# Operand preparation moved about in a fused attention and expert kernel: a second raw-weight buffer, earlier GpSimd sums, other places for copies out and late forms, six staging tiles

## The chip, the cores and the metric

The kernel runs on one core of a Trainium2 chip, as one program that is launched once. The metric is the device time of that launch in microseconds. The kernel before was run three times: 1815.36, 1820.99 and 1821.14 us, median 1820.99.

The engines are named as in the profile: PE is TensorE (matrix products), DVE is VectorE, ACT is ScalarE, POOL is GpSimd, and SP is SyncE, which here issues nearly all DMAs. Each engine works through its own instruction list in order.

## The reference

A gated linear attention makes x, and a mixture of experts over x makes the output. Every expert is applied to every token; the gate is normalised over rows and columns in eight iterations.

```python
# attention: q, k, v, a_re, a_im are [4, 8, 768, 48]
for t in range(S):
    S_re, S_im = ar * S_re - ai * S_im + k[t] (x) v[t], ar * S_im + ai * S_re
    y[t] = q[t] @ S_re
x = y, reordered to [3072, 384]

# experts: N = 3072 tokens, D = 384, E = 8, F = 1024
P = exp(x @ w_gate - max)
for _ in range(8):
    P /= P.sum(1, keepdims=True) + 1e-9
    P /= P.sum(0, keepdims=True) + 1e-9
    P *= N / E
out = sum over e of P[:, e:e+1] * (relu(x @ w1[e]) @ w2[e])
```

## The kernel before, in words

**Stages.** Phase 1 (to about 541 us) makes x in twelve blocks of 256 tokens by the attention, and runs experts 0 and 1 on each block behind it (matmul lines L234 and L207 to L209). A short tail to 645 us (`phase2a`) ends those experts, does the first three iterations of the gate, and prepares the first two weight sets for phase 2b. Phase 2b, from 645 us to the end, runs experts 2 to 7 over all tokens, and nearly all of the change is there.

**The steps of phase 2b.** The 3072 tokens are four groups u of 768. The six experts have 48 hidden chunks of 128; three chunks make one weight set t, so there are 16 sets, and 64 steps n, one for each pair of group and set: u = n // 16, and m is the number of the step within its group. Even groups walk the sets upward, odd ones downward.

**One step.** The first layer is a scheme of 15 block products in place of 18 (`prod`, matmul lines L1052 to L1054, three matmuls of 384 columns each, in a high and a low part for precision). Its token operands are 15 forms (`P1` to `P15`: sums and differences of token blocks), and its weight operands are in four tiles `wa`, `wb`, `wc`, `wd`. Products go to PSUM banks X, Y, Z, V and P (X and P take turns in one pair of buffers, Y, Z and V in another). A finished bank is copied by ACT (`copy`, L1062) or added by DVE (`add`, L1065) into the partial results "11", "12", "21", "22" (that one stays in its bank), "31" and "32". Then come the relus: ACT writes the high part (L1070), DVE the low part `hl` (L1071). Between the products stand the 18 units of the second layer, which belong to the step before (`unit`, matmul lines L1005 to L1007, three matmuls each). `fill(s)`, s from 0 to 14, stands after each product and holds units, jobs for that place (`todo`), jobs of the late forms (`xjobs`), and one job of `fin`. A step has 99 matmuls.

**The banks of the second layer.** The units write six accumulators (`po`) for the token chunks k = 0 to 5. When an expert ends for a group, each accumulator is added into the output tile `oa` by a job of `finish` (by ACT at L984 and L986 for the first expert of a group, by DVE at L988 otherwise), which is put in `fin`; the last expert's job also stores the tile (L990: to `od`, or to the output). `fin` gives up one job at each of the fills 0 to 7, 10 and 11.

**Weights.** In the group u = 0 the sets are made on the fly: `raw_w` loads raw weights (L819, 1152 KB), `sums` forms their sums with 12 groups of operations on GpSimd (L828), and `prep_w` splits each tile into a high part (ACT, L865) and a low part (DVE, L869) and stores it to DRAM (L871). There is one raw tile and one sum tile. In step m the raw load of set m + 2 is issued at fill 6, the sums of set m + 2 at fill 7; the tiles of set m + 1 are split at fills 0 to 5, `wa` (from sums) at 3. Groups u of 1 or more reload the finished sets (`load_set`, L851), all four tiles at fill 0.

**Forms.** The forms of groups 0 and 1 are made during phase 1 (`forms_early`, through two staging tiles `xst`), those of groups 2 and 3 during the steps of group u - 1 (`forms_late`, in steps of n = 16 on and 32 on). A list of jobs does it: `plain` (eight DMAs from `x_d` to `xf`, L767), loads (two DMAs each, L739, into `xb` and `xt`), `full` (DVE, L743), sums (DVE, L749), high part (ACT, L755), low part and store (DVE and SP, L760 and L761). Late jobs are taken at fills 1, 3 and 5 of a step. `swap` (L810) reloads one form of the next group as soon as the last product of the old one has used it.

**Ends of a step.** The relu of "31" for the third chunk is put off into the next step: `carry` (L1092) runs ACT's and DVE's part after the first product.

Notation in code: `SUB` = 256, `TH` = 384 (a half of a group's tokens), `C` = 384, `TRI` = 3, `NS` = 3, `NT` = 16, `NU` = 4. The order of instructions on each engine is that in which the code is written and the fills are emptied; DMAs of SP are issued in that order, and at most eight are under way at a time.

Of the kernel before, what the change touches and what calls it, by code (L numbers as in the profile page):

```python
# [18 lines left out]
CH = 128  # L19
# [53 lines left out]
class Net:  # L73
# [707 lines left out]
    def forms_early(self):  # L781
        tmp, G = self.tmp, NCT * NCH
        T = [tmp.tile([128, G, CH], F32, tag="t1", name=f"xt{k}", bufs=5).rearrange("p (j s) t -> p j (s t)", j=2) for k in range(5)]
        sq = tmp.tile([128, 2, G, CH], F32, tag="sq", name="xst", bufs=1).rearrange("p a (j s) t -> p a j (s t)", j=2)
        temps = [T[3][:, 0], T[3][:, 1], T[4][:, 0]]
# [12 lines left out]
    def forms_late(self, u, pool):  # L798
        n = [0]

# [4 lines left out]
        return self.forms(u, lambda c, j: pool.tile([128, TH], F32, tag=f"xb{c}{j}", name=f"xb{c}{j}_{u}"), temp,  # L805
# [6 lines left out]
    def raw_w(self, t):  # L812
        raw = self.raw = self.wr.tile([128, TRI, 2 * C], F32, tag="raw", name=f"raw{t}")
# [8 lines left out]
    def sums(self, t):  # L822
        G = self.nc.gpsimd
        R = self.raw.rearrange("p f (c d) -> p f c d", d=128)
        s = self.sum = self.wr.tile([128, 11, 128], F32, tag="sum", name=f"sum{t}")
# [17 lines left out]
    def ring(self, t):  # L843
        W = self.W[t] = {nm: self.wp.tile([128, 2, 6, 128], F32R, tag="w", name=f"{nm}{t}_{self.nring}") for nm in ("wa", "wb", "wc", "wd")}
        self.nring += 1
        return W

    def load_set(self, t):
        W = self.ring(t)
        for q, nm in enumerate(("wa", "wb", "wc", "wd")):  # L850
            self.nc.sync.dma_start(W[nm].bitcast(F32).rearrange("p a b c -> p (a b c)"), self.wd[t][:, q])  # L851

    def prep_w(self, t):
        nc, V, A = self.nc, self.nc.vector, self.nc.scalar
        R = self.raw.rearrange("p f (c d) -> p f c d", d=128)
        W, s = self.ring(t), self.sum
        parts = {}

        def part(name, nm, pieces):
            w = W[nm]  # L860
            po = [([w[:, h, k] if k is not None else w[:, h].rearrange("p (a b) d -> p a b d", a=2) for h in range(2)], src) for k, src in pieces]

            def hi():
                for o, src in po:
                    A.activation(o[0], src, AF.Copy)  # L865

            def lo():
# [3 lines left out]
                nc.sync.dma_start(self.wd[t][:, q], w.bitcast(F32).rearrange("p a b c -> p (a b c)"))  # L871

            parts[name] = (hi, lo)

        part("wd", "wd", [(None, R[:, 1:3, 3:6])])
        part("wc", "wc", [(slice(0, 5), R[:, 0, 1:6]), (5, R[:, 1, 0])])
        part("wa", "wa", [(slice(0, 6), s[:, 0:6])])
        part("wb", "wb", [(5, R[:, 1, 2]), (slice(0, 5), s[:, 6:11])])
        return parts

    def phase2a(self, c2):
# [7 lines left out]
        self.W, self.X, self.nring = {}, {}, 0  # L889
# [14 lines left out]
        self.raw_w(0)  # L904
        self.sums(0)
# [5 lines left out]
        for k in range(HEAD):  # L911
# [3 lines left out]
            if k < 2:  # L915
                prepare(k)
                self.raw_w(k + 1)
            if k == 0:
                self.sums(1)
        more(len(todo))  # L920
        self.moe.send((None, None, None))

    def phase2b(self, c2):
# [22 lines left out]
        def rescale(u, k):  # L946
            tt = tile_of(u, k)
            A.activation(oa[tt], oa[tt], AF.Copy, scale=self.P[:, tt, 2:3])

        def early(u, k):  # L950
# [8 lines left out]
            def job():  # L959
                r = o if u == 0 else oa[tt]  # L960
# [14 lines left out]
        def finish(u, e, k):  # L975
# [4 lines left out]
            def job():  # L980
                if e == e0:
                    oa[tt] = self.xa.tile([128, C], F32, tag=f"oa{k}", name=f"oa{tt}")
                    if u == 0:
                        A.activation(oa[tt], p, AF.Copy)  # L984
                    else:
                        A.activation(oa[tt], p, AF.Copy, scale=self.P[:, tt, e:e + 1])  # L986
                else:
                    V.scalar_tensor_tensor(oa[tt], p, self.P[:, tt, e:e + 1], oa[tt], ALU.mult, ALU.add)  # L988
                if e == e1:
                    nc.sync.dma_start(self.od[k] if u == 0 else self.out[tt * CH:tt * CH + CH, :], oa[tt])  # L990
# [21 lines left out]
        for n, (u, t) in enumerate(steps):  # L1012
# [54 lines left out]
            def hh(i, j, src):  # L1067
                t = [self.hp.tile([128, TH], F32R, tag=f"h{q}{i}{j}", name=f"h{q}{i}{j}_{n}") for q in "hl"]
                h[i, j] = t
                A.activation(t[0], src, AF.Relu)  # L1070
                return lambda: V.scalar_tensor_tensor(t[1], src, 0.0, t[0].bitcast(F32), ALU.max, ALU.subtract)  # L1071

            def fill(s):
# [5 lines left out]
                if u and s in (1, 3, 5) and m < NT - 1 and xjobs:  # L1079
# [3 lines left out]
                if s < 8 or s in (10, 11):  # L1083
# [31 lines left out]
            l01 = hh(0, 1, c["12"])  # L1115
# [10 lines left out]
            hh(1, 1, bank["X"])()  # L1126
# [3 lines left out]
            l00 = hh(0, 0, c["11"])  # L1130
# [4 lines left out]
            l10 = hh(1, 0, c["21"])  # L1135
# [4 lines left out]
            l21 = hh(2, 1, c["32"])  # L1140
# [10 lines left out]
        carry.pop(0)()  # L1151
# [180 lines left out]
```

## Time and profile before

| what | value |
|---|---|
| runs before | 1815.36, 1820.99, 1821.14 us (median 1820.99) |
| profiled execution | 1818.91 us, span 1817.1 us, mean granted TensorE clock 0.987 |
| end of phase 1, start of phase 2b | about 541 us, 645.72 us |
| step 0 of phase 2b | 645.72 to 660.66 us |
| group u = 0, steps 1 to 15 | 660.66 to 948.06 us |
| u = 1, u = 2, u = 3 | from 948.06, 1234.81 and 1522.15 us |
| matmuls | 11774, PE busy 1742.1 us |
| DMA | 346.03 MB, mean 190 GB/s |

How to read it: steps are told apart by their last product's matmuls, and the start of a step is that of its first product. A row of waits gives the instruction that waited, by its engine, tile and line, then `<-` and what released it, then the sum, the number and the longest of these waits. A row of windows gives the start and end, the length, the busy time (and count of instructions) of PE, weight loads, DVE, ACT and POOL, then the granted clock, the share of the DMA engines and GB/s. A row of the timeline gives start, duration, engine, line, operation, tiles and, in brackets, idle time and its releaser.

### The profile page before, as it was taken

The numbers are of one execution on the slowest core, as the hardware profiler recorded it, in microseconds if no ns is written. First come the engines' busy times: TensorE is split into PE (matmuls) and PEld (weight loads), VectorE is DVE, ScalarE is ACT, GpSimd is POOL, SyncE is SP. The second block draws the span as 40 slices with busy tenths as digits, with TensorE's granted clock in tenths as the row PEclk, the third lists the DMA queues.
The fourth block names the chain that finished last, engine by engine and source line by source line (L and its number), as shares of the span: only waits on it lengthen the run. The fifth ranks groups of instructions, "written<-read, shape, count | busy, mean of one in ns | idle before, by whom it ended". The sixth has DMA issues, their size and how long they took to land.

```text
span 1817.1 us, 31284 instructions
## 1 busy us (share of the span) xinstructions
PE 1742.1 (96%) x11774; PEld 1690.6 (93%) x11774; DVE 1289.1 (71%) x2710; ACT 746.5 (41%) x1673; POOL 219.3 (12%) x360
## 2 busy tenths in 40 slices
PE   6999999999999989999999999999999999999998
PEld 4888899999999978899998999999999999999998
DVE  7888999998886678877765566655566655556554
ACT  7544444554544544444432433332433333333332
POOL 3101111111110144335310000000000000000000
PEclk9999999999999999999999999999999999999999
DMA  7435444543457855666667666667656746455550
GB/s 218 120 92 144 115 100 125 161 111 110 117 152 237 333 219 202 236 231 235 243 231 243 227 236 246 211 203 251 222 209 217 233 176 226 174 183 210 192 195 31
DMA packets 160831, 346.03 MB, mean 190 GB/s; under 512 B 15264, under 2 KB 101536, under 8 KB 160672
## 3 DMA queue, kind: packets, MB, share of 16 engines
q1 hardware_dynamic: 155264, 334.03, 53.8%
q0 software_dynamic: 4608, 9.52, 2.1%
q8 instruction: 95, 1.56, 0.3%
q14 instruction: 64, 0.52, 0.1%
q10 hardware_dynamic: 800, 0.39, 0.1%
HBM read 232.53 MB, written 98.70 MB: 182 GB/s over the span
## 4 chain that ended last, share of the span: by engine, by line
PE 74%; DVE 10%; DMA 6%; POOL 4%; ACT 3%; issue 2%; SPq 1%; DVEq 0%; ACTq 0%; POOLq 0%
PE ph L234 9%; PE po L1005 9%; PE po L1007 9%; PE po L1006 9%; POOL sum L828 4%; DMA raw<-in_w_dram 4%; PE po L207 3%; PE po L209 3%; PE po L208 3%; PE X L1052 3%; PE X L1054 3%; PE X L1053 3%; PE sp L577 2%; PE Y L1052 2%; PE Y L1053 2%; PE Y L1054 2%
## 5 line engine op out<-in xcount | busy, mean ns | idle before, releaser
L1005 PE MATMUL po<-wd,hh 128*128 128x384 f32 x768 | 258.3, 336 | 7.4 <-DVE oa L988 3.4
L1007 PE MATMUL po<-wd,hl 128*128 128x384 f32 x768 | 257.9, 336 | 0.0
L1006 PE MATMUL po<-wd,hh 128*128 128x384 f32 x768 | 257.8, 336 | 0.0
L234 PE MATMUL ph<-xh,w 128*128 128x256 f32 x1152 | 228.5, 283 | 4.5 <-ACT hf L247 3.3
L234 PEld LDWEIGHTS ph<-xh,w 128*128 128x128 f32 x1152 | 187.4, 191 | 5.7 <-ACT hf L247 3.8
L246 ACT ACTIVATE hh<-ph 128x256 fp32r<-128x256 f32 x192 | 73.2, 381 | 208.7 <-PE ph L234 207.9
L234 PE MATMUL ph<-xl,w 128*128 128x256 f32 x576 | 155.1, 284 | 1.3 <-DVE xl L647 1.3
L1005 PEld LDWEIGHTS po<-wd,hh 128*128 128x128 f32 x768 | 145.1, 189 | 8.7 <-DVE oa L988 4.0
L1007 PEld LDWEIGHTS po<-wd,hl 128*128 128x128 f32 x768 | 145.0, 189 | 0.4 <-DVE hl L1071 0.2
L1006 PEld LDWEIGHTS po<-wd,hh 128*128 128x128 f32 x768 | 145.0, 189 | 0.0
L207 PE MATMUL po<-w,hh 128*128 128x384 f32 x384 | 141.4, 368 | 0.6 <-ACT yst L212 0.5
L1005 PE MATMUL po<-wc,hh 128*128 128x384 f32 x384 | 130.1, 339 | 6.6 <-ACT oa L986 3.3
L209 PE MATMUL po<-w,hl 128*128 128x384 f32 x384 | 131.1, 342 | 2.7 <-DVE hl L248 2.6
L208 PE MATMUL po<-w,hh 128*128 128x384 f32 x384 | 130.4, 339 | 0.0
L1007 PE MATMUL po<-wc,hl 128*128 128x384 f32 x384 | 129.9, 338 | 0.0
L539 POOL DMA_DIRECT2D qs<-z x144 | 77.0, 541 | 438.0 <-issue 84.3
L1006 PE MATMUL po<-wc,hh 128*128 128x384 f32 x384 | 129.7, 338 | 0.0
L234 PEld LDWEIGHTS ph<-xl,w 128*128 128x128 f32 x576 | 106.8, 191 | 1.8 <-DVE xl L647 1.7
L1070 ACT ACTIVATE hh<-X 128x384 fp32r<-128x384 f32 x64 | 31.5, 492 | 186.2 <-PE X L1054 186.2
L248 DVE TENSOR_TENSOR hl<-hf,hh 128x256 fp32r<-128x256 f32 x192 | 81.0, 423 | 27.8 <-ACT hf L247 26.6
L828 POOL TENSOR_TENSOR sum<-raw 128x128 f32<-128x128 f32 (+1 forms) x96 | 66.3, 721 | 230.5 <-DMA raw<-in_w_dram 145.3
L988 DVE SCALAR_TENSOR_TENSOR oa<-po,P,oa 128x384 f32<-128x384 f32 x120 | 72.9, 612 | 19.6 <-PE po L1007 19.6
(1818 smaller groups left out, 4458.9 us busy)
## 6 DMA issues: line engine op xcount, KB each, us to landing
wd<-wd SPq DMA_DIRECT2D x58, 768.0 KB, 5.7
wa<-wd SPq DMA_DIRECT2D x42, 768.0 KB, 4.3
wb<-wd SPq DMA_DIRECT2D x42, 768.0 KB, 5.7
wc<-wd SPq DMA_DIRECT2D x42, 768.0 KB, 4.4
xP<-xf SPq DMA_DIRECT2D x60, 384.0 KB, 4.8
raw<-in_w_dram SPq DMA_DIRECT2D x12, 1152.0 KB, 7.9
wd<-wc SPq DMA_DIRECT2D x16, 768.0 KB, 3.5
wd<-wa SPq DMA_DIRECT2D x16, 768.0 KB, 3.9
```

Source lines behind the costliest of these rows:

```text
L207: nc.tensor.matmul(po[k], hh[:, s], w2h, start=f == 0, stop=False)
L208: nc.tensor.matmul(po[k], hh[:, s], w2l, start=False, stop=False)
L209: nc.tensor.matmul(po[k], hl[:, s], w2h, start=False, stop=f == NF - 1)
L234: nc.tensor.matmul(ph, w[:, k, ct * 128:ct * 128 + 128], x[:, ct, :], start=q == 0, stop=q == len(terms) - 1)
L248: nc.vector.tensor_tensor(hl, hf, hh.bitcast(F32), ALU.subtract)
L828: G.tensor_tensor(o, a, b, op)
L1005: nc.tensor.matmul(po[k], hh[:, s], w2[0], start=c == 1, stop=False)
L1006: nc.tensor.matmul(po[k], hh[:, s], w2[1], start=False, stop=False)
L1007: nc.tensor.matmul(po[k], hl[:, s], w2[0], start=False, stop=c == NF)
L1052: nc.tensor.matmul(ps, w[:, 0, k], x[:, 0], start=start, stop=False, skip_group_check=True)
L1053: nc.tensor.matmul(ps, w[:, 0, k], x[:, 1], start=False, stop=False, skip_group_check=True)
L1054: nc.tensor.matmul(ps, w[:, 1, k], x[:, 0], start=False, stop=True, skip_group_check=True)
```

## The change

1. `forms_early` stages through six tiles: the two of `xst` and four that lie in tiles of the attention's input pool.
2. `forms_late` keeps the six loaded blocks in one tile `xb`. During u = 0, when there are no late forms, the slot of that tile holds the raw weights of the odd sets from t = 3 on: a second raw buffer. The raw weights of set 1 go to the place of the output tile, before that is used.
3. Raw weights are asked for a step sooner: sets 0 and 1 at the start of phase 2a, set 2 there after the sums of set 1, set 3 in step 0, and set m + 3 at fill 5 of step m. The sums of set m + 2 are issued at fill 5 of step m (7 before).
4. `prep_w` for set m + 1: the high part of `wd` is made at fill 12 of the step before, and the others stand one fill earlier than before. A slot of the ring of weight tiles is taken where its high part is made.
5. `oa` is one tile for the six chunks of a group, not one for each chunk.
6. `carry`: the relu of "31" is issued after the copy of "11" in place of before that of "12", and its low part after the first `add`.
7. `fin` gives up a job at fill 12 as well.
8. Late forms: no job at fills 1, 3 and 5 of a group's first step (m = 0); the first three jobs (`plain` and two loads) come at its fill 14, the rest from m = 1 on.

```diff
     def forms_early(self):
...
+        qk = self.ain.tile([128, 2, G, CH], F32, tag="qk", name="xsu", bufs=1).rearrange(...)
+        z = self.ain.tile([128, 2, G, ZW], F32, tag="z", name="xsv").rearrange(...)[...]
+        stages = [t[:, a] for t in (sq, qk, z) for a in range(2)]
...
-            return sq[:, n[1] % 2].bitcast(F32R)
+            return stages[n[1] % len(stages)].bitcast(F32R)
...
     def forms_late(self, u, pool):
+        x = pool.tile([128, 2 * NCT, TH], F32, tag="xb", name=f"xb{u}")
...
-        return self.forms(u, lambda c, j: pool.tile([128, TH], F32, tag=f"xb{c}{j}", name=f"xb{c}{j}_{u}"), temp,
+        return self.forms(u, lambda c, j: x[:, 2 * c + j], temp,
...
-    def raw_w(self, t):
-        raw = self.raw = self.wr.tile([128, TRI, 2 * C], F32, tag="raw", name=f"raw{t}")
+    def raw_w(self, t, pool=None):
+        if t == 1:
+            raw = self.xa.tile([128, 2 * NS, C], F32, tag="oa", name=f"raw{t}").rearrange(...)
+        elif pool is None:
+            raw = self.wr.tile([128, TRI, 2 * C], F32, tag="raw", name=f"raw{t}")
+        else:
+            raw = pool.tile([128, 2 * NCT, TH], F32, tag="xb", name=f"raw{t}").rearrange(...)
+        self.raw[t] = raw
...
         self.raw_w(0)
+        self.raw_w(1)
         self.sums(0)
...
                 prepare(k)
-                self.raw_w(k + 1)
             if k == 0:
                 self.sums(1)
+                self.raw_w(2)
...
             if u == 0 and 1 <= m < NT - 1:
-                parts = self.prep_w(m + 1)
-                for nm, a, b in (("wd", 0, 1), ("wc", 1, 2), ("wa", 3, 4), ("wb", 4, 5)):
-                    todo.setdefault(a, []).append(parts[nm][0])
+                for nm, a, b in (("wd", None, 0), ("wc", 0, 1), ("wa", 2, 3), ("wb", 3, 4)):
+                    if a is not None:
+                        todo.setdefault(a, []).append(parts[nm][0])
                     todo.setdefault(b, []).append(parts[nm][1])
+            if n == 0:
+                self.raw_w(3, xb)
             if u == 0 and m + 2 < NT:
-                if m:
-                    todo.setdefault(6, []).append(lambda t=m + 2: self.raw_w(t))
-                todo.setdefault(7 if m else 0, []).append(lambda t=m + 2: self.sums(t))
+                parts = self.prep_w(m + 2)
+                todo.setdefault(12, []).append(parts["wd"][0])
+                todo.setdefault(5 if m else 0, []).append(lambda t=m + 2: self.sums(t))
+                if m and m + 3 < NT:
+                    todo.setdefault(5, []).append(lambda t=m + 3: self.raw_w(t, xb if t % 2 else None))
...
-                if u and s in (1, 3, 5) and m < NT - 1 and xjobs:
+                if u and s in (1, 3, 5) and 0 < m < NT - 1 and xjobs:
                     xjobs.pop(0)()
                     if len(xjobs) > 3 * (NT - 2 - m):
                         xjobs.pop(0)()
-                if s < 8 or s in (10, 11):
+                if u and m == 0 and s == 14 and xjobs:
+                    for _ in range(3):
+                        xjobs.pop(0)()
+                if s < 8 or s in (10, 11, 12):
                     if fin:
                         fin.pop(0)[1]()
...
             prod("P1", "X", True)
             copy("12", "X")
-            while carry:
-                carry.pop(0)()
             fill(0)
             prod("P2", "Y", True)
             copy("11", "Y")
+            l20 = carry.pop(0)() if carry else None
             fill(1)
             prod("P4", "X")
             add("11", "X")
+            if l20:
+                l20()
             fill(2)
```

SP's list where the steps 15, 16 and 17 meet, before (`xP` are swapped forms, `xf` and `x_d` the forms and blocks in DRAM, `od` the stored output tiles):

```order
L810 DMA xP_1_11863<-xf_160 128x768
L767 DMA xf_161<-x_d_93 128x3x128 x8
L739 DMA xb_2_11909<-x_d_93 128x3x128
L739 DMA xt_1_11910<-x_d_93 128x3x128
L739 DMA xb_2_11928<-x_d_93 128x3x128
L739 DMA xt_2_11929<-x_d_93 128x3x128
L990 DMA od_166<-oa_9453 128x384
L990 DMA od_167<-oa_9467 128x384
L990 DMA od_168<-oa_9480 128x384
L851 DMA wa_16_12056<-wd_156 128x1536
```

and of the change:

```order
L814 DMA xP_1_11860<-xf_160 128x768
L1003 DMA od_166<-oa_9462 128x384
L1003 DMA od_167<-oa_9462 128x384
L1003 DMA od_168<-oa_9462 128x384
L1003 DMA od_163<-oa_9462 128x384
L767 DMA xf_161<-x_d_93 128x3x128 x8
L739 DMA xb_11869<-x_d_93 128x3x128
L739 DMA xt_1_12034<-x_d_93 128x3x128
L739 DMA xb_11869<-x_d_93 128x3x128
L739 DMA xt_2_12037<-x_d_93 128x3x128
L861 DMA wa_64_12050<-wd_156 128x1536
```

The eight plain DMAs and the four loads have moved behind four stores of finished tiles, the fourth of which (`od_163`, chunk 0) belongs to fill 12 of step 16.

DVE's list at the start of step 16, before (L1071 is the low part of a relu, L743 a `full` of the late forms, L988 a copy out, L1065 an `add`):

```order
L1071 SCALAR_TENSOR_TENSOR hl_15_11868<-31_15_11732,hh_15_11867 128x384
L1065 TENSOR_TENSOR 11_16_11896<-11_16_11896,X_11882 128x384
L743 TENSOR_TENSOR xb_2_11909<-xb_2_11909,xt_1_11910 128x384
L988 SCALAR_TENSOR_TENSOR oa_9453<-po_0_3_11595,P,oa_9453 128x384
L988 SCALAR_TENSOR_TENSOR oa_9467<-po_0_4_11606,P,oa_9467 128x384
L743 TENSOR_TENSOR xb_2_11928<-xb_2_11928,xt_2_11929 128x384
L988 SCALAR_TENSOR_TENSOR oa_9480<-po_0_5_11615,P,oa_9480 128x384
L1065 TENSOR_TENSOR 31_16_11923<-31_16_11923,X_11882 128x384
```

and DVE's list from the late part of step 16 into step 17 with the change (L1091, L1001 and L1082 are the lines that were L1071, L988 and L1065):

```order
L1091 SCALAR_TENSOR_TENSOR hl_16_11985<-11_16_11892,hh_16_11984 128x384
L1001 SCALAR_TENSOR_TENSOR oa_9462<-po_0_0_11638,P,oa_9462 128x384
L1082 TENSOR_TENSOR 32_16_11929<-32_16_11929,V_12004 128x384
L1091 SCALAR_TENSOR_TENSOR hl_16_11997<-21_16_11919,hh_16_11996 128x384
L1082 TENSOR_TENSOR 31_16_11909<-31_16_11909,V_12004 128x384
L1091 SCALAR_TENSOR_TENSOR hl_16_12011<-32_16_11929,hh_16_12010 128x384
L1001 SCALAR_TENSOR_TENSOR oa_9462<-po_0_1_11649,P,oa_9462 128x384
L743 TENSOR_TENSOR xb_11869<-xb_11869,xt_1_12034 128x384
L743 TENSOR_TENSOR xb_11869<-xb_11869,xt_2_12037 128x384
L1001 SCALAR_TENSOR_TENSOR oa_9462<-po_0_2_11662,P,oa_9462 128x384
L1082 TENSOR_TENSOR 11_17_12064<-11_17_12064,X_12040 128x384
L1091 SCALAR_TENSOR_TENSOR hl_16_12022<-31_16_11909,hh_16_12021 128x384
```

Both `full` have moved from step 16, one on each side of two copies out, to the start of step 17, ahead of that step's first `add`, and the copy out of chunk 0 has moved from step 17 into step 16.

More of the change, by code (lines that the diff above doesn't have):

```diff
@@ L823, in sums @@
         G = self.nc.gpsimd
-        R = self.raw.rearrange("p f (c d) -> p f c d", d=128)
-        s = self.sum = self.wr.tile([128, 11, 128], F32, tag="sum", name=f"sum{t}")
+        R = self.raw[t].rearrange("p f (c d) -> p f c d", d=128)
+        s = self.sum[t] = self.wr.tile([128, 11, 128], F32, tag="sum", name=f"sum{t}")
         def tt(o, a, b, op=ALU.subtract):
@@ L841, in sums, with ring, part @@
         tt(s[:, 10], s[:, 10], s[:, 5])
-    def ring(self, t):
-        W = self.W[t] = {nm: self.wp.tile([128, 2, 6, 128], F32R, tag="w", name=f"{nm}{t}_{self.nring}") for nm in ("wa", "wb", "wc", "wd")}
+    def ring(self, t, nm):
+        W = self.W.setdefault(t, {})
+        W[nm] = self.wp.tile([128, 2, 6, 128], F32R, tag="w", name=f"{nm}{t}_{self.nring}")
         self.nring += 1
-        return W
+        return W[nm]
     def load_set(self, t):
-        W = self.ring(t)
         for q, nm in enumerate(("wa", "wb", "wc", "wd")):
-            self.nc.sync.dma_start(W[nm].bitcast(F32).rearrange("p a b c -> p (a b c)"), self.wd[t][:, q])
+            self.nc.sync.dma_start(self.ring(t, nm).bitcast(F32).rearrange("p a b c -> p (a b c)"), self.wd[t][:, q])
     def prep_w(self, t):
         nc, V, A = self.nc, self.nc.vector, self.nc.scalar
-        R = self.raw.rearrange("p f (c d) -> p f c d", d=128)
-        W, s = self.ring(t), self.sum
+        R = self.raw[t].rearrange("p f (c d) -> p f c d", d=128)
         parts = {}
-        def part(name, nm, pieces):
-            w = W[nm]
-            po = [([w[:, h, k] if k is not None else w[:, h].rearrange("p (a b) d -> p a b d", a=2) for h in range(2)], src) for k, src in pieces]
+        def part(nm, pieces):
+            po = []
             def hi():
+                w = self.ring(t, nm)
+                po.extend(([w[:, h, k] if k is not None else w[:, h].rearrange("p (a b) d -> p a b d", a=2) for h in range(2)], src()) for k, src in pieces)
                 for o, src in po:
@@ L870, in lo @@
                 q = ("wa", "wb", "wc", "wd").index(nm)
[L871 to L878, printed above, removed]
+                nc.sync.dma_start(self.wd[t][:, q], self.W[t][nm].bitcast(F32).rearrange("p a b c -> p (a b c)"))
+            parts[nm] = (hi, lo)
+        part("wd", [(None, lambda: R[:, 1:3, 3:6])])
+        part("wc", [(slice(0, 5), lambda: R[:, 0, 1:6]), (5, lambda: R[:, 1, 0])])
+        part("wa", [(slice(0, 6), lambda: self.sum[t][:, 0:6])])
+        part("wb", [(5, lambda: R[:, 1, 2]), (slice(0, 5), lambda: self.sum[t][:, 6:11])])
         return parts
@@ L888, in phase2a @@
         self.wr = c2.enter_context(tc.tile_pool(name="wr", bufs=1, side="right"))
-        self.W, self.X, self.nring = {}, {}, 0
+        self.W, self.X, self.raw, self.sum, self.nring = {}, {}, {}, {}, 0
         self.xa = xa
@@ L981, in job @@
                 if e == e0:
-                    oa[tt] = self.xa.tile([128, C], F32, tag=f"oa{k}", name=f"oa{tt}")
+                    if u not in oa:
+                        oa[u] = self.xa.tile([128, 2 * NS, C], F32, tag="oa", name=f"oa_{u}")
+                    oa[u, k] = oa[u][:, k]
                     if u == 0:
-                        A.activation(oa[tt], p, AF.Copy)
+                        A.activation(oa[u, k], p, AF.Copy)
                     else:
-                        A.activation(oa[tt], p, AF.Copy, scale=self.P[:, tt, e:e + 1])
+                        A.activation(oa[u, k], p, AF.Copy, scale=self.P[:, tt, e:e + 1])
                 else:
-                    V.scalar_tensor_tensor(oa[tt], p, self.P[:, tt, e:e + 1], oa[tt], ALU.mult, ALU.add)
+                    V.scalar_tensor_tensor(oa[u, k], p, self.P[:, tt, e:e + 1], oa[u, k], ALU.mult, ALU.add)
                 if e == e1:
-                    nc.sync.dma_start(self.od[k] if u == 0 else self.out[tt * CH:tt * CH + CH, :], oa[tt])
+                    nc.sync.dma_start(self.od[k] if u == 0 else self.out[tt * CH:tt * CH + CH, :], oa[u, k])
             return k, job
@@ L1069, in hh, with low @@
                 h[i, j] = t
+                return lambda: low(t, src)
+            def low(t, src):
                 A.activation(t[0], src, AF.Relu)
@@ L1125, in phase2b @@
             prod("P12", "X")
-            hh(1, 1, bank["X"])()
+            hh(1, 1, bank["X"])()()
             fill(10)
@@ L1150, in phase2b @@
                 unit(*units.pop(0))
-        carry.pop(0)()
+        carry.pop(0)()()
         last = steps[-1]
```

16 lines of the change are left out of this document (10 added, 6 removed).

## The prediction, made before the changed kernel ran

> **What bounds the kernel now.** I read the page first: busy times, then the chain that ended last.
>
> ```profile
> PE 1742.1 (96%) x11774; PEld 1690.6 (93%) x11774; DVE 1289.1 (71%) x2710; ACT 746.5 (41%) x1673; POOL 219.3 (12%) x360
> PE 74%; DVE 10%; DMA 6%; POOL 4%; ACT 3%; issue 2%; SPq 1%; DVEq 0%; ACTq 0%; POOLq 0%
> ```
>
> TensorE is busy for 96% of the span, and the change leaves its matmuls and their order alone. So only time that PE loses can be won. The windows of busy time by stage show where it is lost.
>
> ```profile
> 645.72:660.66 14.94, 9.78 (x47) 7.49 (x46) 10.12 (x18) 7.88 (x16) 2.72 (x5) 1.00 0.80 296
> 660.66:948.06 287.40, 272.64 (x1506) 261.96 (x1506) 221.74 (x396) 129.49 (x262) 111.27 (x165) 0.99 0.60 227
> 948.06:1024.83 76.77, 71.17 (x389) 69.58 (x388) 42.53 (x82) 26.09 (x52) 0.00 (x0) 0.96 0.73 241
> 1024.83:1144.96 120.13, 120.13 (x695) 120.09 (x695) 77.19 (x149) 40.94 (x82) 0.00 (x0) 1.00 0.66 234
> 959.20:966.00 6.80, 5.85 (x18) 5.85 (x19) 3.52 (x8) 1.01 (x2) 0.00 (x0) 0.50 0.88 307
> ```
>
> The fourth row is seven undisturbed steps: 120.13 / 7 = 17.16 us a step, and with 99 matmuls 0.1733 us each. Two matmuls at the edges of a window count in both neighbours. Against that price step 0 (45 matmuls, 7.8 us) lost 7.1 us, steps 1 to 15 (1504, 260.7 us) about 26.5, and steps 16 to 19 (387, 67.1) 9.7. The fifth row is the price of a drop in the granted clock: 6.8 us at 0.50, so 3.4 us lost after a stall. What the stalls are, the waits of PE say, first in 560:960, then from 960 to the end.
>
> ```profile
> PE X L1052 <- ACT 12_6_10021 L1062: 2.6, 1, 2.6
> PE ph L234 <- ACT hf L247: 2.4, 1, 2.4
> PE po L1005 <- ACT oa L984: 2.4, 1, 2.4
> PE X L1052 <- ACT 12_0_8910 L1062: 2.3, 1, 2.3
> PE po L1005 <- DVE oa L988: 1.8, 1, 1.8
> PE X L1052 <- ACT 21_8_10441 L1062: 1.3, 1, 1.3
> ...
> PE X L1052 <- ACT 21_9_10633 L1062: 0.3, 1, 0.3
> ...
> PE po L1005 <- ACT oa L986: 5.0, 3, 1.7
> PE po L1005 <- DVE oa L988: 4.9, 3, 1.6
> PE X L1052 <- DVE 31_32_14695 L1065: 3.7, 1, 3.7
> PE X L1052 <- DVE 31_16_11923 L1065: 3.6, 1, 3.6
> ACT wa L865 <- POOL sum L828: 10.2, 8, 2.0
> ```
>
> The last row is from ACT's waits in u = 0: eight times ACT stands at `wa`, because the sums aren't done, and PE then waits for a copy behind it. So there are three kinds of loss that the change touches: copies late behind `wa`, second-layer units that wait for a copy out (`po`), and the two starts of u = 1 and u = 2.
>
> **Term 1: steps 1 to 15, +11.4 us.** Sums two fills earlier on raw weights a step older, and `wa` one fill earlier: a set's sums take about 8 us (POOL's 111.27 us in u = 0 for 14 sets), and by the order of the fills those of set m + 2 then run from about 6.5 us to 14.5 us of step m, and `wa` is reached about 20 us after that step's start, so ACT's 10.2 us of waits go. PE's waits on copies other than step 6's (eight rows, from 1.3 down to 0.3 us, 4.9 us together) go with them, and so do the two `po` waits, 2.4 + 1.8, since fill 12 releases one more accumulator. About 4 us more is refilling after these stalls and the half clock after the first `po` wait. 4.9 + 4.2 + 4.3 = 13.4. The 2.6 us of step 6 stay: six rescales (ACT) stand ahead of its copy, unmoved.
>
> ```profile
> 760.02 3.13 ACT L948 ACTIVATE oa<-oa,P 128x384 f32<-128x384 f32 x6
> L1071 DVE SCALAR_TENSOR_TENSOR hl<-31_8_10432,hh 128x384 fp32r<-128x384 f32 x1 | 1.1, 1092 | 0.0
> L1071 DVE SCALAR_TENSOR_TENSOR hl<-11_8_10410,hh 128x384 fp32r<-128x384 f32 x1 | 0.6, 557 | 0.0
> L1071 DVE SCALAR_TENSOR_TENSOR hl<-X,hh 128x384 fp32r<-128x384 f32 x15 | 8.4, 557 | 15.1 <-ACT hh L1070 15.1
> ```
>
> Against it stands a cost. In step 8 the `hl` of "31" ran while GpSimd summed and took 1092 ns; that of "11", at a time when it did not, 557; and those that read a PSUM bank always about 557. Mid-step sums will now meet the low parts of "12", "11" and perhaps "21": 0.53 us each, two or three in each of 13 steps, 14 to 21 us of DVE. DVE is busy 221.74 of 287.40 us, so most of it falls into gaps; I take 2 us of PE (bounds -1, since the old meetings at the step's end go, and 21). 13.4 - 2.0 = 11.4.
>
> The Trainium skill, page "SBUF — State Buffer", section "Who interferes with whom", has a VectorE instruction with two SBUF inputs and a GpSimd one that reads SBUF shut each other out for a whole instruction. The rows agree (1092 against 557 ns); taken as if nothing hid it, this term would be 13.4 - 21 = -7.6, which is the second rival.
>
> **Term 2: step 0 and the tail, +1.8 us.** Its largest wait, 2.3 us for the copy of "12", is for ACT, which had the relu of `carry` and split tiles ahead of it; one to two such pieces move away. I take 2.3 (bounds 0 and 5), and -0.5 for the tail, where `wa` of set 1 still waits for sums.
>
> **Term 3: copies out at fill 12, +12.9 us.** The last accumulator that unit 17 needs was freed at fill 14 only. The clock of the steps that follow two of these waits:
>
> ```profile
> 1450.38:1469.11 18.73, 18.73 (x101) 18.73 (x100) 7.86 (x16) 5.46 (x11) 0.00 (x0) 0.91 0.51 174
> 1731.31:1749.71 18.40, 18.40 (x100) 18.40 (x100) 7.13 (x14) 5.05 (x10) 0.00 (x0) 0.93 0.42 148
> ```
>
> Three waits on ACT (5.0 us) and three on DVE (4.9 us) go, with some 0.1 to 0.3 us of refill each, and with them the two half-clock stretches (18.73 + 18.40 - 2 x 17.16 = 2.8 us). DVE's copy out at fill 12 then stands ahead of the `add` of "32", which I put at 0.35 us each of three times (bounds 0 and 0.6, the length of a copy out). ACT's: 5.8. DVE's: 4.8 + 2.8. Step 48 loses 0.5 for the same reason. Sum 12.9 (bounds 9 and 15).
>
> **Term 4: phase 1, +3 us.** Six staging tiles in place of two.
>
> ```profile
> ACT xst L755 <- DMA xf<-xst: 14.6, 9, 4.4
> 558.47 0.52 ACT L755 ACTIVATE xst<-xt 128x384 fp32r<-128x384 f32 x1 [4.41 <-DMA xf<-xst]
> ```
>
> ACT stood nine times for a staging tile, and the longest of these, 4.41 us, ended just ahead of PE's 2.4 us wait for `hf`. Half clock follows that. With six tiles it goes: 2.4 and a part of 3.4, less what ACT is late with anyway; 3 (bounds 0 and 6).
>
> **Term 5: the starts of u = 1 and u = 2, -10.7 us.** Before, DVE met `full` in step 16, and the loads it needs stood on SP behind eight plain DMAs:
>
> ```profile
> 946.54 5.20 SPq L767 DMA_DIRECT2D xf<-x_d  x8
> 951.78 0.62 SPq L739 DMA_DIRECT2D xb<-x_d  x1
> ...
> 953.77 0.62 SPq L739 DMA_DIRECT2D xt<-x_d  x1
> DMA to landing us min/median/max: 4.3/4.5/4.5
> 957.03 0.56 DVE L743 TENSOR_TENSOR xb<-xb,xt 128x384 f32<-128x384 f32 x1 [5.55 <-DMA xt<-x_d]
> 958.56 0.55 DVE L743 TENSOR_TENSOR xb<-xb,xt 128x384 f32<-128x384 f32 x1
> 959.55 0.54 DVE L1065 TENSOR_TENSOR 31_16_11923<-31_16_11923,X 128x384 f32<-128x384 f32 x1
> 960.15 0.69 PE L1052 MATMUL X<-xP,wb 128*128 128x384 f32 x1 [3.61 <-DVE 31_16_11923 L1065]
> ```
>
> The second pair's last DMA went out at 953.77 and landed 4.5 us later, 11.6 us after the first plain one; PE lost 3.61 us and, by the half clock, 6.6 us in all. In the change SP has all of it behind `od_163`, the store of chunk 0, whose copy out is DVE's at fill 12 of step 16. Where DVE comes to that place an undisturbed step shows, step 48 (begun at 1522.15):
>
> ```profile
> 1536.39 0.55 DVE L1065 TENSOR_TENSOR 32_48_17427<-32_48_17427,V 128x384 f32<-128x384 f32 x1
> 1539.45 1.14 DVE L988 SCALAR_TENSOR_TENSOR oa<-po,P,oa 128x384 f32<-128x384 f32 x2
> ```
>
> The copy out comes in at 1536.39, 14.2 us into the step, takes 0.6, and the store is issued at 14.9. The plain DMAs then start at about 15.2 in place of -1.5 (946.54 against 948.06), and the second pair lands 11.6 us later, 26.8 us after the step's start. Step 16 itself has 90 matmuls: 15.6 us and about 0.9 of small losses, so step 17 starts at 16.5, and its product P7 needs the X bank that `add` "11" of step 17 frees, at 4.2 us of the step: 20.7. But DVE has both `full` ahead of that `add`. It gets through at 26.8 + 0.6 + 0.6 + 0.6 = 28.6 us. PE waits about 8 us, and the half clock costs 3 more (3.4 in the row of the drop). Each of the two starts then loses 0.9 + 11.4 = 12.3 in place of 7.0: 2 x 5.35 = 10.7 us more. Bounds: if the landing is 2 us earlier or later, 4 on each side; if nothing waits, +12.
>
> Queued behind the waiting `full` are the `add`s of step 17 and `hl` of "31"; PE waits for the first of these. Queued on SP behind `od_163` are also the weights of the next step, which have until the end of step 17.
>
> **The sum.** 11.4 + 1.8 + 12.9 + 3.0 - 10.7 = 18.4 us. The profiled execution took 1818.91 us around a span of 1817.1: 1800.5. The median before, 1820.99, lies 2.1 above it, the lowest run 3.5 below; I say 1801. Five single bounds do not all fall on one side: 1788 to 1813 is its own range.
>
> **Rivals.** (a) The late loads are in time, or DVE has slack that I miss, and the stalls at u = 1 and u = 2 go: term 5 becomes +12, so 1818.9 - 18.4 - 22.7 = 1778. For it: no other DMA has to be issued in between, and the loads wait for nothing else. Against it: DVE's order has both `full` ahead of the `add`, and 11.6 us do not fit into 5.5. (b) **Sums at mid-step block DVE** where PE follows it closely: the low parts of "12", "11" and "21" stand between the adds of the Z and P banks, three meetings of 0.53 us in each of 13 steps, 21 us, and a third of these stalls draws half clock, 13 x 1.7 / 3 or some 7. This decides from 18.4 + 2.0 = 20.4 us on; 28 gives 1818.9 - 18.4 - 2 + 28 = 1826.5, slower. For it: 1092 against 557 ns. Against it: DVE has 23% idle there. (c) The sums aren't earlier in fact, because the tile they go to is still being read, and the fill 12 only moves a wait: terms 1 and 3 shrink to a few us, and term 5 eats them: 1816, no difference.
>
> **How the numbers follow.** My forecast has 0.69, (a) 0.13, (b) 0.09, (c) 0.09. The range 1777 to 1814 takes in the forecast with (a), and leaves out (b), (c). A measurement of this kernel can tell 0.3%, 5.5 us, from no change. Faster by more: 0.69 and 0.13, less 0.01 at the forecast's upper edge: 0.81. Same: (c) and that edge, 0.11. Slower: 0.08 of (b).
>
> **What would show it.** Right: ACT's `wa` no longer waits on GpSimd; no `po` wait at fill 14; in steps 17 and 33 a PE wait of some 8 us on DVE's "11", DVE's `full` on a DMA of `x_d`, and a clock drop behind it; `hl` of "12" or "11" near 1.1 us in u = 0. Wrong: PE's wait at step 17 below 4 us or missing (a); PE waits on DVE in most steps of u = 0 (b); ACT's waits on sums unchanged (c).

## The result, and the profile after

The changed kernel took 1798.72 us (median of four runs, 1796.88 to 1801.97) against 1820.44 us before (a fourth run of that kernel included): a ratio of 0.9889, 95% interval 0.9866 to 0.9912, so 1.1% faster. The forecast was 1801 us. Its profiled execution has a span of 1796.8 us, 20.3 less than before. Three executions lie far outside and are left out: one of an experiment's kernel (2407.91 us, at a mean granted clock of 0.655), which was run again, and two of the kernel before (3435.70 and 7740.80 us).

The windows of the changed kernel, for the stretches that were shown of before (step 0, steps 1 to 15, steps 16 to 19, and seven undisturbed steps), and one more:

```profile
648.18:662.34 14.16, 9.75 (x46) 7.45 (x46) 6.65 (x13) 6.22 (x13) 0.00 (x0) 1.00 0.34 111
662.34:928.74 266.40, 263.19 (x1505) 259.65 (x1505) 204.25 (x395) 125.85 (x260) 81.44 (x156) 1.00 0.63 240
928.74:1009.57 80.83, 70.50 (x388) 68.99 (x388) 41.27 (x80) 25.69 (x52) 0.00 (x0) 0.96 0.67 225
1009.57:1129.77 120.20, 120.20 (x694) 120.04 (x694) 78.39 (x153) 40.79 (x83) 0.00 (x0) 1.00 0.68 237
954.08:960.91 6.83, 4.11 (x13) 4.11 (x14) 3.04 (x6) 0.98 (x2) 0.00 (x0) 0.53 1.00 370
```

The price of a step is as before, 120.20 / 7 = 17.17 us. Steps 1 to 15 take 266.40 us in place of 287.40: 21.0 us won. Steps 16 to 19 take 80.83 in place of 76.77: 4.1 lost. GpSimd's operations there take 0.52 us each (81.44 / 156) in place of 0.67 (111.27 / 165), so a set's twelve take 6.3 us in place of 8.1. What is left of PE's waits from step 16 on, the longest four (the six others are of 0.2 to 0.5 us):

```profile
PE X L1069 <- DVE 11_33_14826 L1082: 8.4, 1, 8.4
PE X L1069 <- DVE 11_17_12064 L1082: 7.3, 1, 7.3
PE X L1069 <- DVE 32_17_12113 L1082: 2.4, 1, 2.4
PE V L1069 <- DVE 32_32_14691 L1082: 0.5, 1, 0.5
...
```

No wait on a copy out (`po`) is left. New are the two in steps 17 and 33. The timeline of SP around the first of them:

```profile
933.75 10.09 SPq L1003 DMA_DIRECT2D od<-oa  x4
943.89 5.20 SPq L767 DMA_DIRECT2D xf<-x_d  x8
949.19 0.56 SPq L739 DMA_DIRECT2D xb<-x_d  x1
...
951.12 0.62 SPq L739 DMA_DIRECT2D xt<-x_d  x1
```

The fourth of the stores, that of chunk 0, goes out at 943.52. The timeline of DVE there:

```profile
942.88 0.61 DVE L1001 SCALAR_TENSOR_TENSOR oa<-po,P,oa 128x384 f32<-128x384 f32 x1
...
954.08 0.56 DVE L743 TENSOR_TENSOR xb<-xb,xt 128x384 f32<-128x384 f32 x1 [7.69 <-DMA xt<-x_d]
955.20 0.56 DVE L743 TENSOR_TENSOR xb<-xb,xt 128x384 f32<-128x384 f32 x1 [0.57 <-DMA xt<-x_d]
955.68 0.61 DVE L1001 SCALAR_TENSOR_TENSOR oa<-po,P,oa 128x384 f32<-128x384 f32 x1
956.20 0.54 DVE L1082 TENSOR_TENSOR 11_17_12064<-11_17_12064,X 128x384 f32<-128x384 f32 x1
```

This is the forecast chain: the copy out of chunk 0 at 942.88 (14.1 us into step 16, which began at 928.74), its store as the last of the four, the first plain DMA at 943.89, DVE idle 7.69 us for the loads, then the `add` on which PE waited. The window 954.08 to 960.91 above has a granted clock of 0.53.

The order of the matmuls is the same in both kernels, so the start of one matmul in two traces gives the lead of one over the other at that place. By that account, term for term:

| term of the forecast | forecast, us | measured, us |
|---|---|---|
| 1: steps 1 to 15 | +11.4 | +21.0 |
| 2: step 0; tail | +2.3; -0.5 | +0.8; -1.5 at the gate's chain, +0.3 elsewhere |
| 3: copies out at fill 12 (steps 18 to 61 without 32, 33) | +12.9 | +12.9 |
| 4: phase 1 | +3.0 | +4.2 near 559 us, -2.2 near 592 us |
| 5: steps 16, 17, 32, 33 | -10.7 | -10.9 (79.46 to 90.34 us) |
| end of the program (steps 62 and 63, and what follows) | 0 | -1.1 |
| before 541 us, where nothing was changed | 0 | -3.2 |
| sum | +18.4 | +20.3 |

Of the -1.1, 1.0 stands behind the last matmul: from its start to the end of the program it is 6.5 us before and 7.2 to 7.8 us in all twelve changed kernels. What does that was not tried.

### The profile page after: what moved, and what is told of

It reads as the page before. It is cut to its first block, busy times and chain, and to the rows that moved or that the text cites. A ratio compares the mean times of both kernels' runs of the same rounds, so it can differ in the third digit from the quotient of the medians.

```text
span 1796.8 us, 31293 instructions
## 1 busy us (share of the span) xinstructions
PE 1728.0 (96%) x11774; PEld 1683.8 (94%) x11774; DVE 1270.7 (71%) x2710; ACT 738.6 (41%) x1673; POOL 191.7 (11%) x360
## 4 chain that ended last, share of the span: by engine, by line
PE 79%; DVE 12%; DMA 4%; ACT 2%; issue 2%; SPq 1%; DVEq 0%; ACTq 0%
PE po L1020 10%; PE po L1018 10%; PE po L1019 10%; PE ph L234 8%; PE X L1069 4%; PE X L1071 3%; PE X L1070 3%; PE po L207 3%; PE po L209 3%; PE po L208 3%; PE Y L1069 2%; PE Y L1071 2%; PE Y L1070 2%; PE sp L577 2%; DMA xt<-x_d 2%
## 5 line engine op out<-in xcount | busy, mean ns | idle before, releaser
L1001 DVE SCALAR_TENSOR_TENSOR oa<-po,P,oa 128x384 f32<-128x384 f32 x120 | 73.2, 614 | 21.1 <-PE po L1020 20.9
L207 PEld LDWEIGHTS po<-w,hh 128*128 128x128 f32 x384 | 73.1, 190 | 8.0 <-issue 4.0
```

Source lines behind the costliest of these rows:

```text
L207: nc.tensor.matmul(po[k], hh[:, s], w2h, start=f == 0, stop=False)
```

## The experiments

A kernel with a single time ran once, beside runs of the kernel before with medians from 1814.67 to 1820.18 us, so the argument goes by the steps and not by these times. A step "loses" the time from one matmul's start to the next beyond 0.173 us, summed over its delays of more than 0.05 us.

### Where the late loads stand

```diff
-                if u and m == 0 and s == 14 and xjobs:
+                if u and m == 0 and s == 12 and xjobs:
```

> The changed kernel, but the three first late jobs (plain and two loads) stand at fill 12 of a group's first step, ahead of the copy out of chunk 0 at the same fill, in place of fill 14, behind it. DVE's order stays. Theory (SP held by the store of chunk 0): SP issues them about 10 us sooner, both pairs land before or just as step 17 needs them, the PE waits of 7.3 and 8.4 us on 11_17 and 11_33 and the half clock behind them go; steps 17 and 33 lose at most 1 to 3 us each (before: 12.7 and 10.5), time 1776 to 1782. Rival (the transfers are late anyway, held by other DMAs in flight): the two waits stay over 4 us and the time over 1790.

It took 1781.99 us (1779.07 to 1782.65), ratio to before 0.9791 (0.9773 to 0.9808). SP's timeline in it, with the plain DMAs, two of the four weight tiles and the read of `od` that matter below, and that read's time to landing:

```profile
933.78 5.20 SPq L767 DMA_DIRECT2D xf<-x_d  x8
...
942.75 0.43 SPq L861 DMA_DIRECT2D wa<-wd  x1
...
944.27 0.62 SPq L861 DMA_DIRECT2D wd<-wd  x1
...
947.29 0.47 SPq L968 DMA_DIRECT2D od<-od  x1
...
DMA to landing us min/median/max: 10.1/10.1/10.1
```

and DVE's, with the two `full` and the next operation that waited for a DMA:

```profile
944.56 0.56 DVE L743 TENSOR_TENSOR xb<-xb,xt 128x384 f32<-128x384 f32 x1 [0.58 <-DMA xt<-x_d]
945.66 0.56 DVE L743 TENSOR_TENSOR xb<-xb,xt 128x384 f32<-128x384 f32 x1 [0.55 <-DMA xt<-x_d]
...
957.40 1.27 DVE L973 SCALAR_TENSOR_TENSOR od<-y,P,od 128x384 f32<-128x384 f32 x2 [5.63 <-DMA od<-od]
```

The plain DMAs go out at 933.78, 7.5 us after step 16's start at 926.33, in place of 15.2, and DVE waits 0.58 and 0.55 us for the loads, not 7.69. Step 33 loses nothing (10.5 in the changed kernel). So it is where the loads stand in SP's list, behind the store of chunk 0 or ahead of it, that made the two waits; nothing else was altered. Step 17 still loses 6.4 us, by another wait: DVE's `early` job reads back chunk 0 of group 0 from `od`. That read was issued at 947.29 and landed at 957.37, 10.1 us later. The store that it reads back had landed at 946.15. Four weight tiles of 768 KB, issued from 942.75 to 944.27, went ahead of it and landed from 949.00 to 955.38. In the kernel before, those four were spread over 10 us by waits for their ring slots, and the read landed 2.5 us after its issue (975.09 to 977.63). The expectation (1 to 3 us a step) missed this second wait, which the changed kernel has too (2.4 us in step 17). The Trainium skill, page "DMA: Bandwidth & Descriptors", section "Queues, rings and completion order", says that each DMA engine consumes one issuer's descriptors in the order of its ring; the landings here came in the order of issue.

Then the late jobs where they stood before (the edit takes out the `0 <` of the condition at fills 1, 3 and 5, and the three jobs at fill 14):

> The changed kernel with late jobs as before: at fills 1, 3 and 5 of the first step too, none at fill 14. Theory: the wait of the kernel before returns in steps 16 and 32 (3.6 us, with half clock some 6.5 lost in each), none in 17 and 33: 24.7 us lost there becomes 14, time about 1787 to 1790. Rival (the waits of steps 17 and 33 come from the copy out at fill 12 on DVE, not from where the loads stand): steps 17 and 33 still lose over 5 us each, time about 1800 or more.

The same kernel, run again:

> The same kernel as the run with late jobs as before, whose one execution showed a mean clock of 0.655. Expectation as there: steps 16 and 32 lose about 6.5 us each, 17 and 33 under 3, time 1787 to 1790.

1785.86 us. Steps 16 and 32 lose 6.2 and 8.2 us, 17 and 33 lose 1.8 and 0.0. The old wait is back, and the copy out at fill 12 alone does no harm there. In these four steps together 16.2 us are lost, against 24.7 in the changed kernel and 8.0 with the late jobs at fill 12. So, with the copy out at fill 12, moving the late jobs to fill 14 cost 8.5 us, and moving them to the place ahead of that copy out would have won 8.2.

### The copy out at fill 12, and carry

```diff
-                if s < 8 or s in (10, 11, 12):
+                if s < 8 or s in (10, 11):
```

> The changed kernel without a copy out at fill 12. Theory: the po waits return in steps 19, 27, 35, 43, 51 and 59 (1.6 us each, 1.8 to 2.5 lost, with two half-clock stretches 15 us in all) and some in u = 0 (steps 3 and 11, 2 to 5 us); but the store of chunk 0 stands behind the late jobs, so SP isn't held and the waits of steps 17 and 33 go (-20 us or more): about 1794, steps 17 and 33 under 3 us each. Rival (those waits don't hang on that store): they stay and the time is about 1815.

1789.73 us. PE's waits from 660 us on:

```profile
PE po L1018 <- DVE oa L1001: 6.6, 4, 1.6
PE X L1069 <- DVE 32_17_12113 L1082: 2.5, 1, 2.5
PE X L1069 <- DVE 11_17_12062 L1082: 2.3, 1, 2.3
PE X L1069 <- DVE 11_33_14824 L1082: 1.4, 1, 1.4
...
```

Half of the expectation came true. The waits on DVE's copy out are back, four of 1.6 us (steps 11, 27, 43 and 59 lose 2.1 each), and the two long waits shrink, since the store now stands behind the late loads. But none on ACT's copy out: steps 19, 35 and 51 lose 0.4 us, where they lost 1.9 before. The two drops of the granted clock, which the expectation counted with the waits, are not back either. Step 17 still loses 8.2, over the 3 that were expected, by the read back of `od` and the loads. With half of term 3 unexplained, carry was undone. (In the kernel before, unlike what its description says, ACT's part of the put-off relu was in fact issued at the end of the step, ahead of the copy of "12"; only DVE's part stood behind the next step's first product.)

```diff
+            while carry:
+                carry.pop(0)()
             fill(0)
...
-            l20 = carry.pop(0)() if carry else None
...
-            if l20:
-                l20()
...
-            carry.append(hh(2, 0, c["31"]))
+            carry.append(hh(2, 0, c["31"])())
...
```

> The changed kernel with the put-off relu of 31 where it was: ACT's part at the end of a step, ahead of the copy of 12, the low part ahead of the first add. Theory (carry matters only where ACT or DVE is behind, in u = 0): steps 1 to 15 lose 7 to 12 us in place of 6.5, later steps the same; time 1800 to 1806. Rival (carry carries the gain of u = 0): steps 1 to 15 lose over 15 us, time over 1808.

1798.84 us; steps 1 to 15 lose 8.9 us in place of 6.5, and 19, 35 and 51 still nothing. So both were undone together:

> The changed kernel without a copy out at fill 12 and with carry where it was. Each of the two undone alone left steps 19, 35 and 51 at 0.4 us or less, where the kernel before lost 1.94 in each. Theory (either one is enough there: with carry put off, ACT has no relu of 31 ahead of the copy out at fill 14; with fill 12, that copy isn't late): with both undone the waits on ACT return, 1.9 us lost in each of steps 19, 35 and 51, beside the 2.0 to 2.1 in 27, 43, 59. Rival (another edit took them away, such as one tile for the output): steps 19, 35 and 51 stay under 0.5.

1796.70 us (the late loads are early here too), and from step 16 on:

```profile
PE po L1018 <- ACT oa L999: 5.0, 3, 1.7
PE po L1018 <- DVE oa L1001: 4.9, 3, 1.6
...
```

These are the two rows of the kernel before, to the digit; steps 19, 35 and 51 lose 1.9 each. So either edit alone takes away ACT's three waits. DVE's need fill 12.

The windows of the steps 44 and 60, which follow two of DVE's waits, show what did not come back:

```profile
1430.18:1447.37 17.19, 17.19 (x101) 17.19 (x100) 7.87 (x16) 5.46 (x11) 0.00 (x0) 1.00 0.56 191
1709.24:1726.43 17.19, 17.19 (x101) 17.19 (x100) 7.14 (x14) 5.05 (x10) 0.00 (x0) 1.00 0.47 166
```

In the kernel before the same two steps, behind waits of the same 1.6 us, ran at 0.91 and 0.93 and took 2.8 us more. So that drop of the clock does not follow from a wait of that length: of these six waits it came behind two before, and behind none here. What decides it, these runs don't show.

### What made u = 0 faster

In the kernel before, GpSimd's longest wait in u = 0 was for the raw weights:

```profile
POOL sum L828 <- DMA raw<-in_w_dram: 113.5, 10, 15.0
```

Raw weights asked for when they were before, and the sums at their old fill, with both buffers kept:

```diff
...
-            if n == 0:
-                self.raw_w(3, xb)
...
-                todo.setdefault(5 if m else 0, []).append(lambda t=m + 2: self.sums(t))
-                if m and m + 3 < NT:
-                    todo.setdefault(5, []).append(lambda t=m + 3: self.raw_w(t, xb if t % 2 else None))
+                if m:
+                    todo.setdefault(6, []).append(lambda t=m + 2: self.raw_w(t, xb if t % 2 else None))
+                todo.setdefault(7 if m else 0, []).append(lambda t=m + 2: self.sums(t))
```

> The changed kernel with both raw buffers, but raw weights asked for when they were before (set m + 2 at fill 6 of step m) and the sums emitted at fill 7. Theory (the gain in u = 0 is that raw weights are there, so that sums begin at 6 us of the step): sums start at about 16 us of the step again, ACT waits at wa, by now a fill earlier, so 2 to 4 us in most steps, and steps 1 to 15 lose 25 us or more (6.0 in the changed kernel, 26.4 before): time 1818 or more. Rival (the gain comes from the other edits, carry, fill 12 and the places of the splits): steps 1 to 15 lose under 12 us, time under 1805.

1815.29 us; steps 1 to 15 lose 21.9 us (25 were expected). Of ACT's waits in u = 0, those on GpSimd are back, the longest:

```profile
ACT wa L875 <- POOL sum L838: 15.3, 10, 2.1
```

and on GpSimd's timeline the sums wait for the raw weights:

```profile
795.81 4.57 POOL L838 TENSOR_TENSOR sum<-raw 128x256 f32<-128x256 f32 x6 [10.14 <-DMA raw<-in_w_dram]
```

That is 16.5 us into its step 7 (begun at 779.32). In the changed kernel ACT has no wait on GpSimd in u = 0 at all, and the sums wait for the sum tile to be read, 6.2 us into step 8 (begun at 788.39):

```profile
794.54 3.11 POOL L838 TENSOR_TENSOR sum<-raw 128x256 f32<-128x256 f32 x6 [10.94 <-DVE wb L879]
```

So 15.4 of the 20.0 us by which the loss in steps 1 to 15 fell (26.5 to 6.5) hang on raw weights being there a step sooner. Undoing carry alone costs 2.4, fill 12 alone 1.5 (8.0 without it), but both together 6.7 (13.1 lost in the run above): here, too, a wait for ACT's copy out, 1.9 us in step 3, comes back only with both undone. The shares overlap, since 15.4 and 6.7 are more than 20.0. The places of the splits and the single output tile were not undone by themselves.

Then the price of sums that meet the low parts: each set's sums computed twice in a row, by a second call of `sums` into the same tile.

> The changed kernel with each set's sums from step 1 on computed twice in a row into the same tile: GpSimd then sums from about 6 to 19 us of a step in place of 6 to 12.4. Theory (a low part that meets the sums takes up to twice its time, but PE is hidden from it, and ready sums have 7 us in hand): the number of slow low parts about doubles, steps 1 to 15 lose at most 6 us more (6.5 to 12), time under 1806. Rival (the meetings are what sets the loss): steps 1 to 15 lose over 15, time over 1808.

1801.40 us; steps 1 to 15 lose 10.0 us, 3.5 more for 13 times 6.3 us of added sums. The low parts of relus from 600 ns up (551 alone) number 29 in steps 1 to 15 before, 13 in the changed kernel, and 46 here. Two of the changed kernel's 13, the slowest and the quickest:

```profile
L1091 DVE SCALAR_TENSOR_TENSOR hl<-12_11_10958,hh 128x384 fp32r<-128x384 f32 x1 | 0.9, 947 | 0.0
...
L1091 DVE SCALAR_TENSOR_TENSOR hl<-12_5_9817,hh 128x384 fp32r<-128x384 f32 x1 | 0.7, 664 | 0.1
```

All 13 are the one of "12", one in each step from 1 to 13. By the time that "11" has its low part, the sums are done.

### The tail and phase 1

The raw weights of set 1 asked for just ahead of its sums, not at the start of the tail:

```diff
         self.raw_w(0)
-        self.raw_w(1)
         self.sums(0)
...
             if k == 0:
+                self.raw_w(1)
                 self.sums(1)
```

> The changed kernel with the raw weights of set 1 asked for after the first set is split, just ahead of the sums of set 1, in place of at the start of the tail. Theory (the sums of set 1 in the changed kernel run beside the gate's chain on DVE, whose operations took up to twice as long at 623 to 631 us, so that PE waited 1.3 us for cs): those operations are short again (L879 wd 0.96, not 1.30; L718 0.18, not 0.43), the wait for cs goes, about 1.5 us won in the tail, with at most 1 lost again in step 0 or 1. Rival (the wait for cs is there anyway): it stays at 1 us or more.

1798.64 us. DVE's timeline for two operations of the tail, in the changed kernel:

```profile
623.36 1.30 DVE L879 TENSOR_TENSOR wd<-raw,wd 128x768 fp32r<-128x768 f32 x1 [0.81 <-ACT wd L875]
628.82 0.43 DVE L718 TENSOR_SCALAR rs<-rs 128x24 f32<-128x24 f32 x1
```

and for the same two with the late load:

```profile
623.78 0.96 DVE L879 TENSOR_TENSOR wd<-raw,wd 128x768 fp32r<-128x768 f32 x1 [0.81 <-ACT wd L875]
626.73 0.18 DVE L718 TENSOR_SCALAR rs<-rs 128x24 f32<-128x24 f32 x1
```

The wait for `cs` is gone and 1.5 us are won there, of which step 0 gives back 0.9 (7.2 lost, 6.3 in the changed kernel; in the last run below, with the same edit, it loses 6.3). So the earlier sums do cost where DVE carries the gate's chain. By the Trainium skill, page "SBUF — State Buffer", section "Who interferes with whom", a VectorE operation with two inputs in SBUF and a GpSimd one that reads SBUF shut each other out; the rows of `wd` agree, 1.30 us with sums beside it, which ran from 622.16 to 630.07 us, against 0.96 without.

Two staging tiles (`stages[n[1] % 2]`):

> The changed kernel with forms_early cycling through two staging tiles. Theory: the stall near 559 us returns (PE waits for hf 2.4 us, with half clock 4 lost), and the ones of the changed kernel near 592 us (yst, 1.9 us) change or go; 1800 to 1803. Rival (six tiles bring nothing because something else is late there): no PE wait over 1 us near 559, time about 1798.

1804.58 us. PE's wait near 559 us is back:

```profile
PE ph L234 <- ACT hf L247: 3.2, 1, 3.2
```

and on ACT's timeline the wait for a staging tile that ended just ahead of it:

```profile
562.57 0.52 ACT L755 ACTIVATE xst<-xt 128x384 fp32r<-128x384 f32 x1 [5.26 <-DMA xf<-xst]
```

With two tiles the lead over before stays the same across 559 us within 0.7 us; each of the eleven kernels with six tiles, the changed one among them, wins 4.0 to 4.2 us there. Near 592 us all of the eleven lose 2.2 to 5.1 us (eight of them with a granted clock of 0.50 for 3.4 us there, the changed kernel without), and this one nothing. There, in the changed kernel, PE waits 1.9 us for ACT's `yst` (L212), which stands behind a high part that waits for DVE:

```profile
592.41 0.52 ACT L755 ACTIVATE xsu<-xt 128x384 fp32r<-128x384 f32 x1 [2.46 <-DVE xt L749]
592.84 0.47 ACT L212 ACTIVATE yst<-po 128x384 f32<-128x384 f32 x1
```

So the gain is given back 33 us later, half of it in the changed kernel and all of it in some others: from 550 to 600 us the eleven win between -0.9 and +2.0 us over before, and the one with two tiles 0.7. By these rows ACT, with staging free, runs up to a later job in its list and stands there. Why two tiles cost some 2 us more in the tail and 2.5 more in step 0 was not tried.

### What beats both

Late loads at fill 12, the copy out at fill 13, the read back of `od` a step later, and one rescale at each of fills 0 to 5 (the edit of the late loads is the one shown above):

```diff
-                for k in (3, 4, 5, 0, 1, 2):
-                    rescale(0, k)
-            for uu, ms in ((0, (1, 2, 4, 5, 12, 13)), ...
+                for s, k in enumerate((3, 4, 5, 0, 1, 2)):
+                    todo.setdefault(s, []).append(lambda k=k: rescale(0, k))
+            for uu, ms in ((0, (2, 3, 4, 5, 12, 13)), ...
...
-                if s < 8 or s in (10, 11, 12):
+                if s < 8 or s in (10, 11, 13):
```

> The run with late jobs at fill 12, and three more edits: the copy out at fill 13 in place of 12 (behind the add of 32), the early sums of group 0 read back in steps 2, 3, 4, 5, 12, 13 of the next group in place of 1, 2, 4, 5, 12, 13, and the six rescales of step 6 at fills 0 to 5, one each, in place of all ahead of its first copy. Theory: the waits of V on 32 (0.4 to 0.5 us, 0.7 lost) in steps 11, 16, 27, 32, 43, 48 and 59 go while no po wait comes back (-4.5); step 17 loses under 1 us (6.4 with late jobs at fill 12, all of it DVE waiting for a read of od behind four weight tiles) (-5.5); step 6 loses under 1 (2.9) (-2). Time 1770. Rival for step 17 (DVE waits because the store it reads back is late, whatever else is queued): the wait only moves to step 18, 1775.

1774.27 us (1773.51 to 1775.73), ratio 0.9756 (0.9740 to 0.9773). PE's waits from 925 us to the end:

```profile
PE po L1018 <- DVE oa L1001: 0.6, 3, 0.2
PE X L1069 <- DVE 11_17_12064 L1082: 0.6, 1, 0.6
PE Z L1069 <- DVE 21_28_13998 L1082: 0.4, 1, 0.4
...
```

Step 17 loses 0.9 us and step 18 0.2, as before the edit. The wait has not moved to step 18; and since the store had landed 1.1 us ahead of the read's issue in the run with late jobs at fill 12, it was for the queue and not for the store. Step 6 loses 1.8 (1 was expected). Steps 11, 27, 43 and 59 lose 0.6 to 0.7, as they did with fill 12: the wait of V on "32" has become one on `po`. Last, with the copy out straight behind the `add` of "32", and set 1's raw weights late:

> The combined run with two more edits: the copy out straight behind the add of 32 in place of at fill 13, and the raw weights of set 1 late as in that run. Theory: the po waits of 0.36 to 0.38 us in steps 11, 27, 43 and 59 go (-1.5), 1.5 us won in the tail, 0.9 lost in step 0: 1772, just not told apart from 1774.3 by three rounds. Rival (the copy out there delays the low part of 21 and with it the second layer): new waits of units on hl in these steps, 1776.

1772.09 us (1769.77 to 1774.73), ratio 0.9738 (0.9694 to 0.9783), not told apart from the run before it. The four `po` waits are gone (0.2 lost in each of these steps), and no wait on `hl` came.

## Why the prediction was right, point by point

**Term 5 held in mechanism and size.** Forecast was that the change's own first late jobs would stand behind the store of chunk 0 and make PE wait about 8 us in steps 17 and 33; it waited 7.3 and 8.4. The move of the loads from fill 14 to fill 12, ahead of that store, shows the cause. What the forecast lacked is the second wait of step 17 (2.4 us), of the read behind four weight tiles, which the sum happened to cover.

**Term 1 was mis-sized: +11.4 forecast, +21.0 measured.** The mechanism was right, as the late-raw run shows: ACT's waits on the sums were what set the loss. Three steps of the sum failed. First, the cost of meetings was put at 2 us, for two or three slow low parts in each step; there was one, "12", at 0.66 to 0.95 us, and the 29 slow ones of before in these steps, most of them "31" and "32" at a step's end, went away. By the doubled sums, where 33 more cost 3.5 us, 16 fewer are worth an estimated 1.7 us, so this was rather a gain. Second, "about 4 us more" for refilling and half clock was too little. PE's waits in these steps fell from 14.4 to 2.8 us, while the rest of the lost time fell from 12.1 to 3.7, so by 8.4; the half clock that began at 764.6 us before, behind the wait of step 6, was not counted. Third, the waits on DVE's adds (2.7 us) were left out, and of the "2.6 us of step 6" that were to stay 1.4 stayed; the step went from 5.1 to 2.9 lost. That DVE's adds were late by the slow low parts fits these rows, but was not tested.

**Term 3 held in size, with a reason too few, and in part by luck.** Its 12.9 us came out, but ACT's share has two sufficient causes, fill 12 and carry, and the forecast named one. And 2.8 of the 12.9 are two drops of the clock that the trace of before happened to have: where both edits were undone, the same waits came back without them.

**Term 4 was half the story.** The stall near 559 us went as forecast (+4.2); the new one near 592 us (-2.2), by the same engine's next wait, was not seen. With a net of -0.9 to +2.0 in the eleven kernels, the forecast of +3 was too high.

**Term 2 was too high.** Step 0 won 0.8 of 2.3: its first copy still waits 2.0 us. In the tail the forecast -0.5 named `wa` of set 1; it was DVE's gate chain beside the earlier sums, -1.5.

**The rivals.** That late loads are hidden anyway fell with steps 17 and 33. That mid-step sums block DVE fell by the doubled sums: twice the sums cost 3.5 us. That the sums wouldn't be earlier fell with GpSimd's rows: they do wait for the tile to be read, but only to 6.2 us of the step. That the total came within 2 us is luck: term 1's surplus, 9.6 us, was offset by terms 2, 4 and 5 (3.4 us short), by the 3.2 us of the unchanged first part, and by 1.1 at the end.

## What to carry to other kernels

SP issues in order, and here one store whose data wasn't ready held twelve later DMAs, for two PE waits of 7.3 and 8.4 us. Before a job with loads is put at a new place, look which stores stand ahead of it there, and for small reads, which large loads. When two edits touch the same wait, undo both before one gets the credit. A second buffer that lets a producer run earlier can be worth more than its consumer waited (here 15.4 us of PE for ACT's 10.2 of waits); look then where the freed engine stops next.

## What the runs showed of the hardware

The first 541 us, the same code in all of these kernels, took from 3.1 us less to 3.2 us more than in the trace of before (from one matmul's start to the same one's), nearly all of it before 250 us. Single profiles therefore say nothing of 3 us in the total. Small losses of the same steps repeated within some 0.1 us (steps 27 and 43: 0.71 or 0.72 in every run with the copy out at fill 12); long waits with a drop of the clock behind them did not (step 33: 9.5 to 11.2 us in the six kernels that have the late jobs at fill 14 and the copy out at fill 12).
